# Linear attention feeding an MLP on one core: 128-token chunks cut into 64-token halves with a state between, all attention products on 64x64 tiles

## The chip, the cores and the metric

One core of a Trainium2 chip. TensorE (PE, with PEld for the load of its stationary operand), VectorE (DVE), ScalarE (ACT), GpSimd (POOL) and the DMA queue of SyncE (SP) run side by side and wait for each other by semaphores. The metric is the device time of one execution in microseconds (us), lower is better; the value is the median of the runs.

## The reference

```python
# B, H, S, D = 4, 8, 768, 48; d_model = H*D = 384, d_ff = 2048
for t in range(S):
    cur = einsum('bhd,bhe->bhde', u * k[t], v[t])
    y[t] = einsum('bhd,bhde->bhe', r[t], state + cur)
    state = w[..., None] * state + einsum('bhd,bhe->bhde', k[t], v[t])
x = y as (B*S, H*D)
h = x @ w_in
out = (max(h, 0) + alpha * min(h, 0)) @ w_out
```

## The kernel before

**Attention.** The 768 tokens are cut into C = 6 chunks of L = 128, and the 8 heads into P = 4 pairs; one call of `attention(c, q, at)` treats pair q of chunk c for the four batches. Head g of a pair lies on partitions 64g to 64g+47. r and k (tile `raw`) are loaded transposed and scaled by powers of w (L310). `scores` (L350) makes 8 products of 48 x 128 by 48 x 128, which fill the two banks A0 and A1; ACT writes the diagonal into `base` (L357) and DVE copies the strict triangle of the scores over it under a mask (L361). `out` adds the old state's part (L397, L391 in chunk 1) and the scores' part (L402, L386) in the bank or banks of y, and `state_product` (L411) makes the k-by-v product of the chunk, with which DVE updates the state T (L479). k is scaled for it by `scale_k` (L420). ACT and DVE split y in a rounded part `xh` and the rest `xl` (L444, L445). The fp32 products stand in the trace as two matmul records each: 8 products are 16 records. From chunk 2 on, y lies in two banks, written from four quadrants of the array; in chunks 0 and 1 it is one bank. The last chunk makes no state product.

**MLP.** 96 steps (`STEPS`), each one block of 128 hidden rows (i) of one chunk (c): `m_in` makes 9 products of 128 x 128 by 128 x 512 into a bank `hp` (L492), ACT and DVE make the activation and its split (L498, L499, L502, L503), and `m_out` adds 9 products to the three banks acc0 to acc2 (L523), three steps later. `SEGMENTS` orders them: blocks 0 to 8 of chunk 0, then of chunk 1, then blocks 9 to 15 of both, then chunk after chunk. So steps 0 to 8 each need a new block of weights, step 9 is the first of chunk 1, and step 18 is the next that needs new weights. `weights(i)` turns a block's bits into `wh` and `wl` with ACT (L253, L263) and DVE (L255, L257, L260, L264).

**Order.** Nothing is issued in program order: each piece of work is added to a `Plan` with its engine, an estimated time and a rank, and `in_order` lists the pieces as a list scheduler would start them (lowest rank of those that are ready). The engines then execute that list in order. The rank of attention is `at`, counted in MLP steps: `begins[c] - before + space * q`, with before and space of 9 and 1.4 for chunk 1, 11 and 2.4 for chunk 2, and 16 and 3.5 beyond. `scores` has rank at, `out` and `state_product` one PE piece of rank at + 1. In chunk 1 the masked copy, the splits and the state update have rank -60, that is, they go first. PSUM has 8 banks with fixed roles: two hp, A0, A1, y, and acc0 to acc2.

Of the kernel before, what the change touches and what calls it, by code (L numbers as in the profile page):

```python
# [18 lines left out]
L = 128  # L19
# [4 lines left out]
HI = 64  # L24
# [5 lines left out]
SPACE = {1: (1.4, 9.0), 2: (2.4, 11.0)}  # L30
# [16 lines left out]

class Piece:
    def __init__(self, eng, us, fn, reads, writes, rank, kb):
        self.eng, self.us, self.fn, self.rank, self.kb = eng, us, fn, rank, kb  # L50
        self.uses = [(r, 0) for r in reads] + [(x, 1) for x in writes]
        self.after, self.behind = set(), set()
        self.start = self.end = None


class Plan:
# [3 lines left out]
    def __init__(self):  # L60
        self.pieces, self.groups, self.log = [], {}, {}
# [19 lines left out]
    def in_order(self):  # L81
# [20 lines left out]

        def ready(p):
            t = 0.0
            for q in p.after:
                t = max(t, q.end + (0.0 if q.eng == p.eng else 0.2 if q.eng == "PE" else 0.1))
            for q in p.behind:
                t = max(t, q.start + 0.001)
            return t
# [5 lines left out]
        while any(waiting.values()):  # L115
            t, e = min((max(free[e], min(x[0] for x in ps)), e) for e, ps in waiting.items() if ps)
            at, p = min((x for x in waiting[e] if x[0] <= t + 0.02), key=lambda x: (x[1].rank, number[x[1]]))
            waiting[e].remove((at, p))
# [16 lines left out]
def rwkv_prelu_kernel(ctx: ExitStack, tc, rk, vkr, wP, uP, u, wall, alpha, w, r_all, k_all, v_all, oT):  # L135
# [25 lines left out]
    one, ones, ident = fixed([128, 2], "one"), fixed([128, 128], "ones"), fixed([128, 128], "ident")  # L161
    strict = fixed([128, 128], "strict", U8)
    utab, alph = fixed([128, H, D], "utab"), fixed([128, NF], "alph")
# [3 lines left out]
    wtok, w128, unit = fixed([128, H, D], "wtok"), fixed([112, P], "w128"), fixed([112, 65], "unit")  # L167

    T = [fixed([112, B, D], f"T{m}") for m in range(P)]
# [5 lines left out]
    bank = pb([128, NT], "acc2")  # L175

# [22 lines left out]
    add("POOL", 0.3, lambda: nc.gpsimd.tensor_copy(strict(), ones()), r=[ones], w=[strict], rank=-99)  # L199
    add("DVE", 0.1, lambda: nc.vector.memset(unit(), 0.0), w=[unit], rank=-100)  # L200
# [16 lines left out]
    def token_table():  # L217
        rows, pt = sb([112, P, L], "g", 3), pb([128, P, 2, HI], "A1")
# [4 lines left out]
        for m in range(P):  # L223
            add("PE", 0.15, lambda m=m: nc.tensor.transpose(
                pt()[:, m].rearrange("p g e -> p (g e)")[:, 0:112], rows()[:, m], ident()[0:112, 0:112]),
                r=[(rows, m), ident], w=[(pt, m)], rank=-30)
        add("DVE", 0.4, lambda: nc.vector.tensor_copy(
            wtok().rearrange("p (m g) e -> p m g e", g=2), pt()[:, :, :, 0:D]), r=[pt], w=[wtok], rank=-30)
# [52 lines left out]
    def attention(c, q, at):  # L281
        first, last = c == 0, c == C - 1

        r, k0 = (sb([112, B, L], *(("o", 2) if first and q == P - 1 else ("raw", 6)))
                 for _ in range(2))
        v, k = sb([128, 2 * B, D], "v", 4), sb([128, 2 * B, D], "kk", 3)
        n = 2 * B * D
        early = -99 + 0.1 * q if first else at - 7
        for j, t in enumerate((r, k0)):
# [3 lines left out]
             -98 + 0.2 * q if first else early + 0.1 * q + 0.15)  # L293

        def k_load():
            load(k, lambda: nc.sync.dma_start(k().rearrange("p x e -> p (x e)"), vkr[c, q, :, n:2 * n]), 192,
                 -20 + q if first else early + 0.1 * q + 0.2, [first_v[P - 1]] if first else [])

        if first:
            first_k.append(k0)  # L300
            first_v.append(v)
            if q == P - 1:
                raw_weights(0, -97, [k0])
                raw_weights(1, -95, [v])
        else:
            k_load()


        for j, (t, tab) in enumerate(((r, lambda: W[q]()[:, None, 0:L]), (k0, lambda: W[q]()[:, None, L - 1::-1]))):
            add("DVE", 0.72, lambda t=t, tab=tab: nc.vector.tensor_tensor(  # L310
                out=t(), in0=t(), in1=tab().broadcast_to([112, B, L]), op=ALU.mult),
                r=[W[q]], w=[t], rank=10 * q + j - 90 if first else at - 2)


        cu = sb([128, 2, B], "cu", 2)
        if c < 2:
            prod = sb([112, B, L], "g", 3)
            add("DVE", 0.7, lambda: nc.vector.tensor_tensor(out=prod(), in0=r(), in1=k0(), op=ALU.mult),
                r=[r, k0], w=[prod], rank=10 * q - 88 if first else at - 3)
            sums, cols = (pb([128, 2 * B], "y"), slice(0, 8)) if c else (bank, slice(8 * q, 8 * q + 8))  # L320
            mine = sums if c else (sums, q)

            def c_sum():
                for b in range(B):
                    nc.tensor.matmul(sums()[:, cols][:, 2 * b:2 * b + 2], prod()[:, b], uw()[:, q], start=True,  # L325
                                     stop=True, skip_group_check=True)

            add("PE", 1.0, c_sum, r=[prod, uw], w=[mine], rank=at - 0.2 - 40 * first - 20 * (c == 1))
            add("ACT", 0.2, lambda: nc.scalar.activation(cu(), sums()[:, cols].rearrange("p (b g) -> p g b", g=2), AF.Copy), r=[mine],
                w=[cu], rank=at - 1)  # L330
        else:
            rt = sb([128, 2 * B, D], "rr", 2)
            load(rt, lambda: nc.sync.dma_start(rt().rearrange("p x e -> p (x e)"), vkr[c, q, :, 2 * n:]), 192,
                 early + 0.1 * q + 0.2, [wh[0]])
            add("POOL", 1.2, lambda: nc.gpsimd.tensor_tensor(out=rt(), in0=rt(), in1=k(), op=ALU.mult), r=[k] + ([wh[12]] if c == 2 else []), w=[rt],  # L335
                rank=at - 2)
# [6 lines left out]


        A = [pb([128, B, L], f"A{g}" if not first or q % 2 == 0 else f"acc{g}") for g in range(2)]

        def scores():
            for b in range(B):
                for g in range(2):
                    nc.tensor.matmul(A[g]()[:, b], k0()[half(g), b], r()[half(g), b], start=(b == 0),  # L350
                                     stop=(b == B - 1), skip_group_check=True)

        add("PE", 1.1, scores, r=[r, k0], w=A, rank=10 * q - 90 if first else at)
        base = [sb([128, B, L], "base", 4) for _ in range(2)]
        for g in range(2):
            for b in range(B):
                add("ACT", 0.39, lambda g=g, b=b: nc.scalar.activation(  # L357
                    base[g]()[:, b], ident(), AF.Copy, scale=cu()[:, g, b:b + 1]), r=[cu, ident], w=[(base[g], b)],
                    rank=at - 0.9 if c != 1 else -50)
        for g in range(2):  # L360
            add("DVE", 0.75, lambda g=g: nc.vector.copy_predicated(  # L361
                base[g](), strict()[:, None, :].broadcast_to([128, B, L]), A[g]()), r=[strict, A[g]], w=[base[g]],
                rank=10 * q - 76 + g if first else at - 1.5 if c != 1 else -60)

        U, plain = None, c < 2
        if plain:
            y = pb([112, B, L], "y" if not first or q % 2 == 0 else "hp", 1 if not first or q % 2 == 0 else 2)
            if not first:  # L370
                U = mine = pb([112, B * D], "A0")
        else:
            y = [pb([112, 2 * 2 * L], "y"), pb([112, 2 * L], "A1")]
            U, mine = y[0], (y[0], "U")
            y_of = [(y[0], "y"), y[1]]

        def u_rows(rows):
            return U()[rows].rearrange("p (b e) -> p b e", b=B) if plain else \
                U()[rows, 2 * L:2 * L + B * D].rearrange("p (b e) -> p b e", b=B)

        def out():
            if plain:
                for b in range(B):
                    for g in range(2):
                        rows, x = (slice(0, HI) if g == 0 else half(g)), g * B + b
                        nc.tensor.matmul(y()[rows, b], v().rearrange("p x e -> p (x e)")[  # L386
                            :, x * D:x * D + rows.stop - rows.start], base[g]()[:, b], start=b == 0,
                            stop=first and b == B - 1, skip_group_check=True)
                for b in () if first else range(B):
                    for g in range(2):  # L390
                        nc.tensor.matmul(y()[half(g), b], T[q]()[half(g), b], r()[half(g), b], start=False,  # L391
                                         stop=(b == B - 1), skip_group_check=True)
                return
            for j in range(2):
                for g, o in ((0, 0), (1, 1), (0, 1), (1, 0)):
                    b = j + 2 * (g ^ o)
                    nc.tensor.matmul(y[g]()[half(o), j * L:(j + 1) * L], T[q]()[half(g), b], r()[half(g), b],  # L397
                                     start=(j == 0), stop=False, skip_group_check=True)
            for j in range(2):
                for g, o in ((0, 0), (1, 1), (1, 0), (0, 1)):  # L400
                    b = j + 2 * (g ^ o)
# [355 lines left out]
```

## Time and profile before

| | |
|---|---|
| median of 3 runs | 526.18 us (524.97 to 528.55) |
| profiled execution, span from first to last instruction | 523.0 us |
| the profiled execution's own time | not listed apart; the median lies 3.2 us above its span |
| PE busy | 509.0 us, 97% of the span |
| DVE busy | 321.0 us, 61% |
| ACT busy | 241.8 us, 46% |
| granted TensorE clock, mean | 0.991 |
| chain that ended last | 93% PE; lines L523 and L492 (the MLP) 38% each |

A high share of an engine is an average over stages; which engine sets the end of a stage is read from the stretches of the span and from the chain of work that ended last.

### The profile page before, as it was taken

What the parts mean: (1) busy time and instruction counts of PE and PEld (TensorE: products, weight loads), DVE (VectorE), ACT (ScalarE), POOL (GpSimd) and SP (SyncE); (2) the same over time, 40 slices, a digit from 0 to 9 for tenths busy, and PEclk for the clock granted to TensorE, in tenths of its full rate; (3) what the DMA queues carried; (4) which work ended last, traced back from release to release, by engine and by line L of the source; (5) the groups of instructions that cost most, each with busy time, mean ns of one, the idle gap of its engine ahead of it and who ended that gap; (6) DMA issues with size and microseconds to landing.
All of it is one profiled execution on the core that took longest, in us unless ns stands there. A gap on an engine that the chain in (4) does not pass through costs nothing.

```text
span 523.0 us, 8426 instructions
## 1 busy us (share of the span) xinstructions
PE 509.0 (97%) x3280; PEld 404.2 (77%) x3280; DVE 321.0 (61%) x513; ACT 241.8 (46%) x525; POOL 38.3 (7%) x45
## 2 busy tenths in 40 slices
PE   7989899999999999999999999999999999999995
PEld 6867677888878777877777777877777778888884
DVE  7799899999455866846764655564544443333331
ACT  3756556677455353543452643543534332432222
POOL 1000011001010112110110101120000000000000
PEclk9799999999999999999999999999999999999998
DMA  7964756552131551431211341220020000100001
GB/s 239 265 216 134 227 178 206 190 172 91 65 102 44 173 180 33 150 92 54 60 49 28 114 107 39 63 82 1 35 92 1 1 2 0 61 0 1 0 1 65
DMA packets 24877, 47.22 MB, mean 90 GB/s; under 512 B 4096, under 2 KB 12416, under 8 KB 24832
## 3 DMA queue, kind: packets, MB, share of 16 engines
q1 hardware_dynamic: 24832, 46.62, 28.3%
q8 instruction: 28, 0.46, 0.4%
q14 instruction: 17, 0.14, 0.1%
HBM read 37.96 MB, written 6.29 MB: 85 GB/s over the span
## 4 chain that ended last, share of the span: by engine, by line
PE 93%; DVE 3%; ACT 1%; DMA 1%; issue 1%; SPq 0%; DVEq 0%; ACTq 0%
PE acc L523 38%; PE hp L492 38%; PE A L350 5%; PE y L402 2%; PE y L397 2%; PE y L386 1%; PE A L402 1%; PE y L411 1%; PE acc L583 1%; PE acc L325 1%; DVE raw L310 1%; PE y L391 1%; DMA raw<-rk 1%; PE acc L350 1%; DVE base L361 1%
## 5 line engine op out<-in xcount | busy, mean ns | idle before, releaser
L499 DVE SCALAR_TENSOR_TENSOR g<-hp,alph,g 128x512 f32<-128x512 f32 x96 | 71.9, 749 | 126.8 <-ACT g L498 126.4
L498 ACT ACTIVATE g<-hp 128x512 f32<-128x512 f32 x96 | 57.3, 597 | 160.1 <-PE hp L492 159.7
L492 PE MATMUL hp<-xh,wh 128*128 128x512 f32 x288 | 116.6, 405 | 1.7 <-DMA xh<-xh 1.7
L492 PE MATMUL hp<-xl,wh 128*128 128x512 f32 x288 | 113.9, 396 | 0.0
L492 PE MATMUL hp<-xh,wl 128*128 128x512 f32 x288 | 113.9, 395 | 0.0
L503 DVE TENSOR_TENSOR gl<-g,gh 128x512 fp32r<-128x512 f32 x96 | 67.4, 702 | 39.4 <-ACT gh L502 39.0
L502 ACT ACTIVATE gh<-g 128x512 fp32r<-128x512 f32 x96 | 60.4, 630 | 61.3 <-DVE g L499 61.0
L523 PE MATMUL acc<-gh,wh 128*128 128x512 f32 x288 | 85.1, 402 | 0.1
L523 PE MATMUL acc<-gh,wl 128*128 128x512 f32 x288 | 83.3, 396 | 0.0
L523 PE MATMUL acc<-gl,wh 128*128 128x512 f32 x288 | 83.2, 396 | 0.0
L492 PEld LDWEIGHTS hp<-xh,wh 128*128 128x128 f32 x288 | 54.1, 188 | 16.2 <-issue 2.5
L492 PEld LDWEIGHTS hp<-xl,wh 128*128 128x128 f32 x288 | 54.1, 188 | 13.0
L523 PEld LDWEIGHTS acc<-gl,wh 128*128 128x128 f32 x288 | 54.0, 188 | 13.1
L523 PEld LDWEIGHTS acc<-gh,wl 128*128 128x128 f32 x288 | 54.0, 188 | 13.0
L492 PEld LDWEIGHTS hp<-xh,wl 128*128 128x128 f32 x288 | 54.1, 188 | 11.9
L523 PEld LDWEIGHTS acc<-gh,wh 128*128 128x128 f32 x288 | 52.6, 188 | 13.7 <-ACT gh L502 0.7
L357 ACT ACTIVATE base<-ident,cu 128x128 f32<-128x128 f32 x192 | 60.2, 390 | 1.0 <-DVE cu L341 0.7
L335 POOL TENSOR_TENSOR rr<-rr,kk 128x384 f32<-128x384 f32 x16 | 17.8, 1114 | 312.5 <-DMA kk<-vkr 207.2
L310 DVE TENSOR_TENSOR raw<-raw,W 112x512 f32<-112x512 f32 x46 | 35.3, 786 | 1.7 <-DMA raw<-rk 1.7
L361 DVE COPY_PREDICATED base<-strict,A 128x512 f32<-128x512 uint8 x44 | 30.5, 731 | 4.6 <-ACT base L357 2.5
L350 PEld LDWEIGHTS A<-raw 48*128 48x128 f32 x352 | 22.0, 192 | 7.5 <-issue 6.2
L350 PE MATMUL A<-raw 48*128 48x128 f32 x352 | 26.2, 290 | 0.0
(90 smaller groups left out, 416.5 us busy)
## 6 DMA issues: line engine op xcount, KB each, us to landing
wraw<-wall SPq DMA_DIRECT2D x16, 768.0 KB, 4.5
raw<-rk SPq DMA_DIRECT2D x46, 224.0 KB, 3.6
v<-vkr SPq DMA_DIRECT2D x24, 192.0 KB, 3.7
kk<-vkr SPq DMA_DIRECT2D x24, 192.0 KB, 3.5
rr<-vkr SPq DMA_DIRECT2D x16, 192.0 KB, 2.4
oT<-o SPq DMA_DIRECT2D x12, 256.0 KB, 2.0
oT<-g SPq DMA_DIRECT2D x6, 256.0 KB, 2.5
xh<-xh SPq DMA_DIRECT2D x36, 32.0 KB, 2.0
```

The source lines that it names most:

```text
L310: add("DVE", 0.72, lambda t=t, tab=tab: nc.vector.tensor_tensor(out=t(), in0=t(), in1=tab().broadcast_to([112, B, L]), op=ALU.mult), r=[W[ ...
L335: add("POOL", 1.2, lambda: nc.gpsimd.tensor_tensor(out=rt(), in0=rt(), in1=k(), op=ALU.mult), r=[k] + ([wh[12]] if c == 2 else []), w=[rt] ...
L350: nc.tensor.matmul(A[g]()[:, b], k0()[half(g), b], r()[half(g), b], start=(b == 0), stop=(b == B - 1), skip_group_check=True)
L357: add("ACT", 0.39, lambda g=g, b=b: nc.scalar.activation(base[g]()[:, b], ident(), AF.Copy, scale=cu()[:, g, b:b + 1]), r=[cu, ident], w=[ ...
L361: add("DVE", 0.75, lambda g=g: nc.vector.copy_predicated(base[g](), strict()[:, None, :].broadcast_to([128, B, L]), A[g]()), r=[strict, A[ ...
L402: nc.tensor.matmul(y[g]()[half(o), j * L:(j + 1) * L], v()[:, g * B + b], base[g]()[:, b], start=False, stop=(j == 1), skip_group_check=True)
L492: nc.tensor.matmul(hp(), a[i]()[:, k], x[c]()[:, k], start=(k == 0 and j == 0), stop=(k == NK - 1 and j == 2))
L498: add("ACT", 0.6, lambda: nc.scalar.activation(g(), hp(), AF.Copy), r=[hp], w=[g], rank=n - 100)
L499: add("DVE", 0.75, lambda: nc.vector.scalar_tensor_tensor(out=g(), in0=hp(), scalar=alph()[:, i:i + 1], in1=g(), op0=ALU.mult, op1=ALU.max ...
L502: add("ACT", 0.64, lambda: nc.scalar.activation(gh(), g(), AF.Copy), r=[g], w=[gh], rank=n - 100)
L503: add("DVE", 0.73, lambda: nc.vector.tensor_tensor(out=gl(), in0=g(), in1=gh(), op=ALU.subtract), r=[g, gh], w=[gl], rank=n - 99)
L523: nc.tensor.matmul(banks[k](), a[i]()[:, NK + k], x(), start=(begin and j == 0), stop=(end and j == 2))
```

## The change

Chunk 0 stays as it is. From chunk 1 on, r and k are scaled over 64 tokens, and a chunk is treated as two halves with a state between: the state T0 before the chunk gives the first half's output, T1 = T0 * w^64 + (first half's k-by-v product) the second half's, and only 64 x 64 blocks of scores are made. For a pair and four batches that is 16 products of scores (into A0 and A1, columns 0 to 255), 16 of k by v (into the same banks from column 256; 8 in the last chunk, which needs T1 alone), 16 through the states and 16 through the scores, each on one of four 64 x 64 tiles of the array.

A PE piece `burst(i, was, at)` makes, for the pair ahead (`was`), the products through the states and the half of those through the scores whose row half j equals the head g, and then, for pair i, the k-by-v products and the scores. The other half of the products through the scores ("crossed") writes the same two y banks from the other row half of the array. It is a PE piece of its own, which waits for an ACT instruction that reads two elements of y (`seen`). So a pair's output is made in the next pair's burst. Chunk 1's bursts are 1.5 steps apart from 0.5 on, chunk 2's 3.2 from 17 on, later ones 4 from begins - 18.5 on; the ones of chunks 1 and 2 begin with a burst of products alone, and the last of chunk 1 and of chunk 5 end with one of outputs alone.

The two hp banks, A0, A1 and y become five banks that the scheduler hands out (`Bank`): a burst takes four at once. A second table `whalf` of powers of w over 64 tokens is made at the start (8 ACT copies, 4 transposes on PE, one DVE copy). The masked copies are 128 x 256 in place of 128 x 512, a pair has two state updates (one in the last chunk, which had none), and chunk 1's y is split in four parts of 48 x 256 as in the later chunks, with ranks near at in place of -60. `scale_k` is now done in the last chunk too. `rr` has one buffer in place of two. A first product of a chunk's MLP step waits for all of xh and xl only in chunks 1 to 5.

```diff
+class Bank:
+    def __init__(self, plan, group, bufs):
+        self.plan, self.slot, self.group, self.bufs = plan, None, group, bufs
...
+    plan.banks += [ps.tile([128, NT], F32, name=f"bank{i}") for i in range(5)]
...
+        def soonest(p):
+            if not p.takes:
+                return []
+            return sorted((x, i) for i in range(len(held)) if (x := open_from(i)) is not None)[:len(p.takes)]
...
+    def half_table():
+        rows, pt = sb([112, P, L], "g", 3), psum()
+        for m in range(P):
+            for j in range(2):
+                add("ACT", 0.3, lambda m=m, j=j: nc.scalar.activation(
+                    rows()[:, m, HI * j:HI * (j + 1)], W[m]()[:, L - 1:HI - 1:-1], AF.Copy, scale=W[m]()[:, L:L + 1]), r=[W[m]],
+                    w=[(rows, (m, j))], rank=-21)
...
+            A = [psum() for _ in range(2)]
...
+            def products():
+                kt = k().rearrange("p x e -> p (x e)")
+                for b in range(B):
+                    for j in range(halves):
+                        for g in range(2):
+                            x, s = g * B + b, slice(HI * j, HI * (j + 1))
+                            rows = slice(HI * g, HI * g + (D if g and b else HI))
+                            nc.tensor.matmul(A[j]()[rows, 256 + b * D:256 + (b + 1) * D],
+                                                 kt[s, x * D:x * D + rows.stop - rows.start], v()[s, x],
+                                                 start=(b == 0), stop=False, skip_group_check=True)
...
+                        for j in range(2):
+                            s = slice(HI * j, HI * (j + 1))
+                            nc.tensor.matmul(A[g]()[s, b * HI:(b + 1) * HI], k0()[half(g), b, s], r()[half(g), b, s],
+                                             start=(g >= halves and b == 0), stop=(b == B - 1),
+                                             skip_group_check=True)
+        if before:
+            (c0, q0), r0, v0, base0, *states0 = before
+            y = [psum() for _ in range(2)]
...
+            def through_state():
+                for j, t in enumerate(states0):
+                    for e in range(2):
+                        for g in range(2):
+                            for b in (e, e + 2):
+                                nc.tensor.matmul(where(g, b, j), t()[half(g), b],
+                                                 r0()[half(g), b, HI * j:HI * (j + 1)], start=(j == 0 and e == 0),
+                                                 stop=False, skip_group_check=True)
+
+            def through_scores(crossed):
+                for e in (1, 0) if crossed else (0, 1):
+                    for g in (1, 0) if crossed else (0, 1):
+                        j = g ^ crossed
+                        s = slice(HI * j, HI * (j + 1))
+                        for b in (e + 2, e):
+                            nc.tensor.matmul(where(g, b, j), v0()[s, g * B + b], base0()[s, g, b], start=False,
+                                             stop=(crossed == 1 and e == 0), skip_group_check=True)
...
+        first = add("PE", (0.7 if before else 0.1) + (0.8 if now else 0.1), run, r=uses, w=writes, rank=at)
+        if before:
+
+            seen = add("ACT", 0.2, lambda: nc.scalar.activation(seen_y(), y[1]()[0:1, L + HI - 1:L + HI + 1], AF.Copy),
+                       r=[y[1]], rank=at - 200)
+            seen.soon[first] = 0.75
+            add("PE", 0.3, lambda: through_scores(1), r=[v0, base0], w=y, rank=at - 200)
+        if now:
+            for g in range(2):
+                add("DVE", 0.42, lambda g=g: nc.vector.copy_predicated(
+                    base()[:, g], strict2()[:, None, :].broadcast_to([128, B, HI]),
+                    A[g]()[:, 0:256].rearrange("p (b t) -> p b t", b=B)), r=[strict2, A[g]],
+                    w=[(base, (g, b)) for b in range(B)], rank=at - 0.5)
...
+            for j in range(halves):
+                t = sb([112, B, D], "T", 9)
+                add("DVE", 0.42, lambda t=t, j=j, of=T[q]: nc.vector.scalar_tensor_tensor(
+                    out=t(), in0=of(), scalar=W[q]()[:, L:L + 1], in1=u_rows(A[j], 256), op0=ALU.mult,
+                    op1=ALU.add), r=[A[j], T[q], W[q]], w=[t], rank=at - 0.4)
...
-    for c in range(1, C):
-        space, before = SPACE.get(c, (3.5, 16.0))
-        for q in range(P):
-            at = begins[c] - before + space * q
-            jobs.append((at, 3, lambda c=c, q=q, at=at: attention(c, q, at)))
+    bursts = []
+    for i, (c, q) in enumerate(pairs):
+        at = {1: 0.5 + 1.5 * q, 2: 17.0 + 3.2 * q}.get(c, begins[c] - 18.5 + 4 * q)
+        bursts.append((i, None if c < 3 and q == 0 else i - 1, at))
+        if c == 1 and q == P - 1:
+            bursts.append((None, i, at + 1.5))
+    bursts.append((None, len(pairs) - 1, at + 4))
```

## Rows read from the trace of the kernel before

**Rows 1.** The page: span, busy time of the engines, one transfer (us to landing last).
```profile
span 523.0 us, 8426 instructions
...
PE 509.0 (97%) x3280; PEld 404.2 (77%) x3280; DVE 321.0 (61%) x513; ACT 241.8 (46%) x525; POOL 38.3 (7%) x45
...
xh<-xh SPq DMA_DIRECT2D x36, 32.0 KB, 2.0
```
**Rows 2.** Stretches: length, then busy us (instructions) of PE, PEld, DVE, ACT, POOL.
```profile
28.00:93.00 65.00, 60.44 (x531) 46.73 (x529) 62.26 (x93) 37.46 (x79) 4.66 (x4) 1.00 0.62 200
93.00:131.00 38.00, 38.00 (x165) 30.59 (x164) 37.31 (x54) 27.51 (x51) 2.21 (x2) 1.00 0.43 142
131.00:511.00 380.00, 380.00 (x2347) 301.39 (x2346) 198.69 (x320) 157.59 (x344) 29.64 (x26) 1.00 0.18 56
```
**Rows 3.** DVE in order of time: start us, us, instruction.
```profile
57.87 0.74 DVE L361 COPY_PREDICATED base<-strict,A 128x512 f32<-128x512 uint8 x1 [1.67 <-ACT base L357]
...
89.02 0.55 DVE L255 TENSOR_SCALAR wx<-wx 128x768 uint32<-128x768 uint32 x1
...
90.15 0.94 DVE L264 TENSOR_TENSOR wl<-wx,wh 128x768 fp32r<-128x768 f32 x1
```
**Rows 4.** The chain that ended last, to 95 us: start us, us, what.
```profile
72.60 1.02 PE y L386 x15
...
74.62 0.59 PE A L411 x14
...
90.35 1.09 PE A L350 x16
91.44 3.69 PE hp L492 x15
```
**Rows 5.** The chain, 156 to 165 us, a pair of chunk 2.
```profile
156.86 1.09 PE A L350 x16
157.96 2.29 PE acc L523 x9
...
162.35 0.24 PE y L397
...
163.95 0.45 PE y L411 x14
164.39 0.66 PE acc L523 x2
```
**Rows 6.** The whole chain's longest pieces, on both sides of an output of chunk 5.
```profile
387.19 2.10 PE hp L492 x9
390.88 2.30 PE acc L523 x9
```
**Rows 7.** PE in order of time, the state's part of one pair's output.
```profile
162.43 0.27 PE L397 MATMUL y<-raw,T 48*48 48x128 f32 x1
...
162.45 0.27 PE L397 MATMUL A<-raw,T 48*48 48x128 f32 x1
162.54 0.27 PE L397 MATMUL y<-raw,T 48*48 48x128 f32 x1
```
**Rows 8.** Groups of instructions by line and form: busy us, mean ns of one.
```profile
L361 DVE COPY_PREDICATED base<-strict,A 128x512 f32<-128x512 uint8 x44 | 30.5, 731 | 4.6 <-ACT base L357 2.5 <-PE A L350 2.1
L445 DVE TENSOR_TENSOR xl<-y,xh 48x256 fp32r<-48x256 f32 x32 | 13.5, 421 | 0.5
L445 DVE TENSOR_TENSOR xl<-y,xh 112x512 fp32r<-112x512 f32 x6 | 4.1, 682 | 2.3 <-ACT xh L444 2.3
L479 DVE SCALAR_TENSOR_TENSOR T<-T,w,A 112x192 f32<-112x192 f32 x4 | 1.6, 409 | 0.0
L498 ACT ACTIVATE g<-hp 128x512 f32<-128x512 f32 x96 | 57.3, 597 | 160.1 <-PE hp L492 159.7
L499 DVE SCALAR_TENSOR_TENSOR g<-hp,alph,g 128x512 f32<-128x512 f32 x96 | 71.9, 749 | 126.8 <-ACT g L498 126.4
L329 ACT ACTIVATE cu<-y 128x8 f32<-128x8 f32 x4 | 0.7, 175 | 7.8 <-PE y L325 7.8
```

More of the change, by code (lines that the diff above doesn't have):

```diff
@@ L279, in lower, with splits, refs, to @@
                 add("SP", 0.45, dma, r=[top[name]], w=[(t, (k, g))], rank=-40 if c == 0 else -8, kb=32)
[L281 to L286, printed above, removed]
+    def splits(k, h, l, src, view, out_rows, cols, parts, us, rank):
+        def refs(t):
+            return [(t, (k, p)) for p in parts]
+        def to(t):
+            return t()[out_rows, cols] if k is None else t()[out_rows, k, cols]
+        add("ACT", us, lambda: nc.scalar.activation(to(h), view(), AF.Copy), r=[src], w=refs(h), rank=rank)
+        add("DVE", us + 0.1, lambda: nc.vector.tensor_tensor(out=to(l), in0=view(), in1=to(h), op=ALU.subtract),
+            r=[src] + refs(h), w=refs(l), rank=rank)
+    def x_tiles(c, q):
+        if q == 0:
+            for t, name in ((xh, "xh"), (xl, "xl")):
+                t[c] = sb([128, NK, NT], name, 2, F32R)
+                top[name] = sb([112, NT], name + "0", 1, F32R)
+        return (top["xh"], top["xl"], None) if q == 0 else (xh[c], xl[c], q - 1)
+    def inputs(c, q, r, k0, v, k, early):
         n = 2 * B * D
-        early = -99 + 0.1 * q if first else at - 7
         for j, t in enumerate((r, k0)):
@@ L311, in attention @@
                 out=t(), in0=t(), in1=tab().broadcast_to([112, B, L]), op=ALU.mult),
-                r=[W[q]], w=[t], rank=10 * q + j - 90 if first else at - 2)
+                r=[W[q]], w=[t], rank=10 * q + j - 90)
         cu = sb([128, 2, B], "cu", 2)
[L316 to L323, printed above, removed]
-                for b in range(B):
[L325 to L330, printed above, removed]
+        diagonal(q, r, k0, cu, bank, slice(8 * q, 8 * q + 8), (bank, q), 10 * q - 88, -90.2 + q, -51 + q)
@@ new lines, in first_chunk, with scores @@
+        A = [psum() if q % 2 == 0 else pb([128, NT], f"acc{g}") for g in range(2)]
+        def scores():
+            for b in range(B):
+                for g in range(2):
+                    nc.tensor.matmul(A[g]()[:, b * L:(b + 1) * L], k0()[half(g), b], r()[half(g), b], start=(b == 0),
+                                     stop=(b == B - 1), skip_group_check=True)
+        add("PE", 1.1, scores, r=[r, k0], w=A, rank=10 * q - 90)
+        base = [sb([128, B, L], "gl" if q % 2 else "base", 3) for _ in range(2)]
@@ new lines, in first_chunk, with out @@
+        y = psum()
+        def out():
+            for b in range(B):
+                for g in range(2):
+                    rows, x = (slice(0, HI) if g == 0 else half(g)), g * B + b
+                    nc.tensor.matmul(y()[rows, b * L:(b + 1) * L], v().rearrange("p x e -> p (x e)")[
+                        :, x * D:x * D + rows.stop - rows.start], base[g]()[:, b], start=b == 0,
+                        stop=b == B - 1, skip_group_check=True)
+        add("PE", 1.0, out, r=[v] + base, w=[y], rank=10 * q - 90)
@@ L354, in attention @@
-        base = [sb([128, B, L], "base", 4) for _ in range(2)]
+        base = sb([128, 2, B, HI], "base", 3)
         for g in range(2):
             for b in range(B):
[L357 to L363, printed above, removed]
@@ L367, in attention @@
[L367 to L379, printed above, removed]
@@ L381, in out, with burst @@
-        def out():
-            if plain:
+                add("ACT", 0.32, lambda g=g, b=b: nc.scalar.activation(
+                    base()[:, g, b], ident2(), AF.Copy, scale=cu()[:, g, b:b + 1]), r=[cu, ident2],
+                    w=[(base, (g, b))], rank=at - 0.9)
+        add("DVE", 0.56, lambda: scale_k(k, whalf, q), r=[whalf], w=[k], rank=at - 1.6)
+        return r, k0, v, k, base
+    def burst(i, was, at):
+        now = None if i is None else pairs[i]
+        before = None if was is None else made.pop(was)
+        uses, writes = [], []
+        if now:
+            c, q = now
+            r, k0, v, k, base = prepare(c, q, at)
+            halves = 2 if c < C - 1 else 1
+            A = [psum() for _ in range(2)]
+            uses += [r, k0, v, k]
+            writes += A
+            def products():
+                kt = k().rearrange("p x e -> p (x e)")
+                for b in range(B):
+                    for j in range(halves):
+                        for g in range(2):
+                            x, s = g * B + b, slice(HI * j, HI * (j + 1))
[3 more added lines that the diff above has]
+                                                 start=(b == 0), stop=False, skip_group_check=True)
@@ L383, in out @@
                 for b in range(B):
                     for g in range(2):
[L385 to L401, printed above, removed]
-                    nc.tensor.matmul(y[g]()[half(o), j * L:(j + 1) * L], v()[:, g * B + b], base[g]()[:, b],
-                                     start=False, stop=(j == 1), skip_group_check=True)
@@ L405, in state_product @@
-        def state_product():
-            kt, vt = k().rearrange("p x e -> p (x e)"), v()
-            for b in range(B):
-                for g in range(2):
-                    rows, x = slice(HI * g, HI if g == 0 else HI + D), g * B + b
-                    nc.tensor.matmul(u_rows(rows)[:, b], kt[:, x * D:x * D + rows.stop - rows.start], vt[:, x],
-                                     start=(b == 0), stop=(b == B - 1), skip_group_check=True)
-        def both():
-            out()
-            state_product()
@@ L607, in rwkv_prelu_kernel @@
         table(m)
-    states = [attention(0, q, -50 + q) for q in range(P)]
+    states = [first_chunk(q) for q in range(P)]
     token_table()
```

271 lines of the change are left out of this document (176 added, 95 removed).

## The prediction

> **What bounds the kernel now.** I read the shares first: PE is busy 97% of the span, DVE 61% [rows 1]. An average over stages says little, so the stretches come next [rows 2]. From 131 to 511 us PE is busy 380.00 of 380 us and DVE 198.69: there every TensorE microsecond taken out shortens the kernel. From 93 to 131 PE is full as well, and DVE nearly so (37.31 of 38). From 28 to 93 us both are nearly full, DVE 62.26 and PE 60.44 of 65, and the question is who sets the pace. The weights answer it: DVE ends block 8's conversion at 90.15 + 0.94 = 91.09 [rows 3], and the product of step 8 that needs it starts at 91.44 [rows 4]. So up to step 9 DVE delivers just in time and PE fills the gaps; from there on PE alone sets the end. I treat the two parts apart, with the border at 93 us.
>
> **The part from 93 us on: what a pair costs PE now.** A piece of 9 MLP products takes 2.10 us, and 2.29 or 2.30 when it follows attention [rows 5, 6], so leaving attention costs 0.19. Scores: 1.09 + 0.19 = 1.28. Outputs and state product: from 162.35 to 164.39, 2.04, + 0.19 = 2.23 [rows 5]. That is 3.51 for each of the 12 pairs of chunks 2 to 4. In chunk 5 there is no state product: from 387.19 + 2.10 = 389.29 to 390.88, 1.59, + 0.19 + 1.28 = 3.06 for 4 pairs [rows 6]. Sum 12 x 3.51 + 4 x 3.06 = 54.4; one scores piece stands ahead of 93 us (at 90.35) [rows 4], so 53.1 lie in this part.
>
> **What a pair will cost.** The four-quadrant products show the pattern: three of a round's four records start at 162.43 to 162.45, the next round at 162.54 [rows 7]. Four tiles work at once and a round of 128 columns lasts 0.11. The k-by-v products, with 48 columns on two tiles, end 14 records in 0.45 [rows 5], 0.064 a round; their weights are up to 64 columns wide. A new round (64 columns of each) is not in this trace: half of 0.11 is 0.055, the k-by-v round 0.064; I take 0.06, between them, since the new products share something with each. What comes on top of the rounds now: scores, 8 rounds of two = 0.88, of 1.28, leaves 0.40; outputs and state, 4 x 0.11 + 8 x 0.11 + 8 x 0.06 = 1.80 of 2.23, leaves 0.43. I take 0.40 for each entry and exit. The new pair makes 64 products, 128 records, on four tiles: 8 rounds through the states, 4 + 4 through the scores, 8 for k by v (still 8 in chunk 5, where the half left uses two tiles), 8 for the scores: 32 x 0.06 + 0.40 = 2.32. Sixteen of them and one more entry for the last output alone: 37.5. **Gain 53.1 - 37.5 = 15.6**; with 0.055 it is 18.1, with 0.064 13.5.
>
> **The wait that is added.** The crossed products wait for the ACT read of y, and behind them on PE stand all MLP products. The read may start when 12 rounds are done and have arrived: some 0.2 + 0.72 + 0.27 (the duration of a small product [rows 7]) = 1.2 after the burst's start; such a read takes 0.18 [rows 8], 1.4. The rounds queued ahead of the crossed ones (28) last until 0.2 + 1.68 = 1.9. So 0.5 us of products cover the wait, and an MLP copy of 0.60 that ACT has in hand [rows 8] would overrun it by a tenth only. I take nothing; if the cover fails, or MLP work is listed between the two parts, one more entry of 0.40 is due, at 17 outputs 6.8 us. Behind the read on ACT stand the MLP's copies of hp, at most the same half microsecond.
>
> **Banks.** A burst takes four of the five, so m_in has one hp until y and A are free. A lone hp is free after ACT's and DVE's reads, 0.60 + 0.75 = 1.35 [rows 8], while m_out's 2.10 pass on PE; nothing is lost unless DVE lags by over 0.75. A burst's own DVE reads of PSUM are two masked copies of 128 x 256 (from the slope between 421 and 682 ns over 256 elements, 0.73 - 0.26 = 0.47 each), two state updates of 0.41 and four splits of 0.42, together 3.4 us [rows 8], within a step of 4.2. DVE has 181 us idle from 131 on [rows 2], which also takes the last chunk's extra scaling and updates. The single `rr` buffer is filled, used and freed within one burst's distance; nothing.
>
> **The part up to 93 us.** PE loses work: a pair of chunk 1 now costs 1.28 + (74.62 + 0.59 - 72.60 + 0.19 = 2.80) = 4.08 [rows 4, 5] against 2.32; 4 x 1.76 - 0.40 = 6.6. But DVE sets the pace, and it gets more: per pair the masked copies -0.52, a second state update +0.41, four splits of 0.42 in place of one of 0.68, +1.00 [rows 8]; 0.89 x 4, and the copy of the second table, at most 0.68: +4.2. Against it: 0.55 of block 9's conversion runs here though nobody needs it before step 18, and 1.67 of DVE's idle time hung on a late PE product [rows 3]; PE, now ahead, can make a further m_out (2.10) while it waits. On the other side chunk 1's last splits (4 x 0.42) and the transfer behind them (2.0 [rows 1]) now stand directly before step 9. 4.2 - 0.6 - 1.7 - 2.1 = -0.2, + up to 3.7 less the 2.1 of step 8's own products: +1.4 at the worst of these. I take 0. The ends are -6.6 (DVE does not set the pace after all) and +6 (none of the reliefs comes). The second table's 8 ACT copies find ACT idle 27 of 65 us [rows 2]; the finer wait of step 0 moves nothing that DVE doesn't hold.
>
> **Sum.** 523.0 - 15.6 + 0 = 507.4 us of span. The median of the runs lies 526.18 - 523.0 = 3.2 above this span, so **510.6 us**.
>
> **A rule against it.** Rows 7 show starts on different tiles 0.01 apart. The Trainium skill ("TensorE: Matmul & The Clock Gate", section "Wait — 56ns, not 53.3ns?") says that matmuls never start closer than about 25 ns, however small. By it 128 records would last 3.2 + 0.40 = 3.6 us, and nothing would be won. The starts on different tiles contradict it over three records; over a long row of records no run here shows it.
>
> **The rivals.** (1) *Slower: PE can't feed four small tiles.* In rows 5 and 7 the mean is never below 27 ns a record (four in 0.11), even where starts cluster. If that is a limit of issue and not of the tiles, the pair costs 128 x 0.027 + 0.40 = 3.9 (112 records, 3.4, in chunk 5): 60.9 against 53.1, +8, the early part +1, so 523 + 9 + 3.2 = 535. It decides from (3.51 - 0.40) / 128 = 24 ns a record. For it: no row is below. Against it: in rows 7 a gap of 0.09 follows each cluster, as when tiles are still busy. Chance 0.12. The page's rule above is this rival. (2) *The wait or the banks take part of it back*: the order is written from estimates, and a burst that needs four free banks and an ACT read may leave PE idle or split the burst, 0.4 to 0.8 per output: +7 to +13, 517 to 523. For it: ACT and DVE run MLP work first. Against: half a microsecond of cover. Chance 0.18. (3) *The early part grows* by 6, since DVE is full there: 516.6. Chance 0.12. (4) *The early part shrinks with PE's work*, -6.6: 504. For it: PE is on the chain for most of it. Against: the weights that come 0.35 us ahead of use. Chance 0.13.
>
> **How the numbers follow.** The forecast, 506 to 515, has 0.45. A change of 1%, 5.3 us, is about what a measurement can tell from none. Faster by over 1% (under 520.9): the forecast, (4), (3) less a little and two thirds of (2): 0.45 + 0.13 + 0.11 + 0.12 = 0.81. Within 1%: 0.01 + 0.06 + 0.03 = 0.10. Slower: 0.09, all of (1). The range goes from 500 (rounds of 0.055 with the shorter early part, 510.6 - 2.5 - 6.6 = 501.5) to 524, the upper end of (2); it leaves out (1) and little else.
>
> **What would show it.** After the change, the 32 score records of a pair should take about 0.5 us (four a round) and a whole burst about 2 us, with MLP pieces back to back around it and PE still full from 100 us on; step 9 should begin near 93 us. Records 27 ns apart through the whole burst mean rival 1. PE idle before the crossed products, ended by ACT, or MLP products between a burst and its crossed part, mean rival 2. A first product of steps 8 or 9 that waits for DVE or for the transfer, past 96 us, means rival 3. The prediction would be wrong above all if four tiles share more than the trace's wide rounds let see.

## Result and the profile after

The changed kernel takes **498.68 us** (median of 4 runs, 498.5 to 501.65) against 526.23 (524.97 to 528.55): ratio 0.9486, 95% interval 0.9452 to 0.952. I had forecast 510.6 with 500 to 524: the sign is right, the gain is 27.5 us where I had 15.6 (measured from the median shown before the prediction), and the time lies just below the range. The profiled execution took 498.5 us, 1.8 above its span of 496.7, at a mean granted clock of 0.987 (before 0.991).

The page of the changed kernel, beside [rows 1]:
```profile
span 496.7 us, 11103 instructions
...
PE 477.7 (96%) x4563; PEld 390.2 (79%) x4563; DVE 322.1 (65%) x550; ACT 242.5 (49%) x565; POOL 45.1 (9%) x49
...
PE acc L661 38%; PE bank L628 36%; PE bank L569 2%; PE bank L579 2%; PE bank L550 2%; PE bank L543 2%; DMA wraw<-wall 1%; DVE wx L333 1%; DVE xl L362 1%; DMA raw<-rk 1%; DVE wl L337 1%; DVE wx L330 1%; DVE g L637 1%; PE acc L473 1%; DVE raw L496 1%
```
The lines are new: L628 is `m_in`, L661 `m_out`; a burst is L569 (through the states), L579 (through the scores, the crossed half too), L543 (k by v) and L550 (scores); L592 reads `seen_y`; L598, L605 and L362 are the masked copy, the state update and the split. Over the span PE has 31.3 us less to do, DVE 1.1 more.

The stretches, with the columns of [rows 2] and its first two borders:
```profile
28.00:93.00 65.00, 55.72 (x780) 43.29 (x781) 63.53 (x107) 41.88 (x99) 2.92 (x2) 0.97 0.64 199
93.00:131.00 38.00, 38.00 (x227) 31.09 (x226) 37.38 (x58) 25.36 (x50) 5.08 (x4) 1.00 0.44 141
131.00:485.00 354.00, 354.00 (x3321) 290.89 (x3320) 198.84 (x341) 155.72 (x361) 34.35 (x26) 1.00 0.20 61
```
From 93 us on PE is still busy without a gap, so what TensorE saves there is saved in the end. Up to 93 us PE fell from 60.44 to 55.72, but DVE went from 62.26 to 63.53 and the end of this part hardly moved.

PE in order of time: a wait for a bank, the lone output that ends chunk 1, the first product of step 9 (92.41), a burst of chunk 3, a `m_in`:
```profile
68.84 0.47 PE L628 MATMUL bank<-xh,wh 128*128 128x512 f32 x1 [3.42 <-DVE T L605]
...
83.06 0.66 PE L569 MATMUL bank<-raw,T 48*48 48x64 f32 x32
83.54 0.41 PE L579 MATMUL bank<-base,v 64*48 64x64 f32 x16
84.59 0.44 PE L579 MATMUL bank<-base,v 64*48 64x64 f32 x16 [0.64 <-ACT seen_y L592]
...
92.41 0.40 PE L628 MATMUL bank<-xh,wh 128*128 128x512 f32 x1
...
222.03 0.66 PE L569 MATMUL bank<-raw,T 48*48 48x64 f32 x32
222.52 0.41 PE L579 MATMUL bank<-base,v 64*48 64x64 f32 x16
222.74 0.57 PE L543 MATMUL bank<-v,kk 64*64 64x48 f32 x30
...
223.19 0.60 PE L550 MATMUL bank<-raw 48*64 48x64 f32 x28
...
223.67 0.41 PE L579 MATMUL bank<-base,v 64*48 64x64 f32 x14
224.01 0.97 PE L661 MATMUL acc<-gh,wh 128*128 128x512 f32 x3
224.82 0.85 PE L661 MATMUL acc<-gh,wl 128*128 128x512 f32 x3
225.51 0.86 PE L661 MATMUL acc<-gl,wh 128*128 128x512 f32 x3
226.21 0.40 PE L628 MATMUL bank<-xh,wh 128*128 128x512 f32 x1
226.44 0.39 PE L628 MATMUL bank<-xh,wl 128*128 128x512 f32 x1
226.67 0.39 PE L628 MATMUL bank<-xl,wh 128*128 128x512 f32 x1
```
The burst is 128 records from 222.03 to 224.01 (eight of them in the lines left out), with the crossed part directly behind the scores and no idle time. Only the lone output at 83.06 shows the wait for `seen_y`. The MLP products at 226.21 to 226.67 start 0.23 us apart.

The chain, with pieces that answer to [rows 6]:
```profile
49.54 6.64 DMA wraw<-wall
...
64.26 0.83 DVE wl L337
65.10 0.87 DVE wx L333
66.32 1.18 DVE raw L496 x2
67.50 0.87 DVE wl L337
...
389.72 0.59 PE bank L569 x32
...
391.68 2.29 PE acc L661 x9
393.96 2.04 PE bank L628 x9
396.01 2.06 PE acc L661 x9
```
Up to 90 us mostly DVE and a transfer of weights stand on it. Behind a burst an `m_out` takes 2.29, then 2.04 and 2.06 alternate where all pieces took 2.10 before. **That is the part of the gain that I had not priced.**

### The profile page after: what moved, and what is told of

It reads as the page before. It is cut to its first block, busy times and chain, and to the rows that moved or that the text cites. A ratio compares the mean times of both kernels' runs of the same rounds, so it can differ in the third digit from the quotient of the medians.

```text
span 496.7 us, 11103 instructions
## 1 busy us (share of the span) xinstructions
PE 477.7 (96%) x4563; PEld 390.2 (79%) x4563; DVE 322.1 (65%) x550; ACT 242.5 (49%) x565; POOL 45.1 (9%) x49
## 4 chain that ended last, share of the span: by engine, by line
PE 84%; DVE 8%; ACT 3%; DMA 2%; issue 1%; SPq 0%; DVEq 0%; ACTq 0%
PE acc L661 38%; PE bank L628 36%; PE bank L569 2%; PE bank L579 2%; PE bank L550 2%; PE bank L543 2%; DMA wraw<-wall 1%; DVE wx L333 1%; DVE xl L362 1%; DMA raw<-rk 1%; DVE wl L337 1%; DVE wx L330 1%; DVE g L637 1%; PE acc L473 1%; DVE raw L496 1%
## 5 line engine op out<-in xcount | busy, mean ns | idle before, releaser
L637 DVE SCALAR_TENSOR_TENSOR g<-bank,alph,g 128x512 f32<-128x512 f32 x96 | 72.0, 750 | 110.0 <-ACT g L636 108.5
L636 ACT ACTIVATE g<-bank 128x512 f32<-128x512 f32 x96 | 57.3, 597 | 141.0 <-PE bank L628 139.1
L628 PE MATMUL bank<-xh,wh 128*128 128x512 f32 x288 | 113.6, 395 | 3.4 <-DVE T L605 3.4
L628 PE MATMUL bank<-xh,wl 128*128 128x512 f32 x288 | 112.3, 390 | 0.4 <-DVE wl L337 0.3
L628 PE MATMUL bank<-xl,wh 128*128 128x512 f32 x288 | 112.1, 389 | 0.0
L661 PE MATMUL acc<-gh,wh 128*128 128x512 f32 x288 | 83.6, 397 | 1.6 <-ACT gh L640 1.6
L661 PE MATMUL acc<-gl,wh 128*128 128x512 f32 x288 | 83.2, 396 | 0.0
L661 PE MATMUL acc<-gh,wl 128*128 128x512 f32 x288 | 81.7, 391 | 0.0
L628 PEld LDWEIGHTS bank<-xh,wh 128*128 128x128 f32 x288 | 54.1, 188 | 15.8 <-ACT wx L326 3.8
L628 PEld LDWEIGHTS bank<-xh,wl 128*128 128x128 f32 x288 | 54.1, 188 | 12.6 <-DVE wl L337 1.3
L661 PEld LDWEIGHTS acc<-gl,wh 128*128 128x128 f32 x288 | 54.1, 188 | 12.1
L628 PEld LDWEIGHTS bank<-xl,wh 128*128 128x128 f32 x288 | 54.0, 188 | 11.7
L661 PEld LDWEIGHTS acc<-gh,wl 128*128 128x128 f32 x288 | 53.9, 188 | 11.6
L661 PEld LDWEIGHTS acc<-gh,wh 128*128 128x128 f32 x288 | 52.6, 188 | 13.2 <-ACT gh L640 1.9
L518 ACT ACTIVATE base<-ident,cu 128x64 f32<-128x64 f32 x160 | 41.4, 337 | 1.1 <-DVE cu L513 1.0
L362 DVE TENSOR_TENSOR xl<-bank,xh 48x256 fp32r<-48x256 f32 (+2 forms) x85 | 37.2, 438 | 3.5 <-ACT xh L361 1.7
```

The lines of the kernel that those rows point to most:

```text
L362: add("DVE", us + 0.1, lambda: nc.vector.tensor_tensor(out=to(l), in0=view(), in1=to(h), op=ALU.subtract), r=[src] + refs(h), w=refs(l), r ...
L518: add("ACT", 0.32, lambda g=g, b=b: nc.scalar.activation(base()[:, g, b], ident2(), AF.Copy, scale=cu()[:, g, b:b + 1]), r=[cu, ident2], w ...
L628: nc.tensor.matmul(hp()[:, :], a[i]()[:, k], x[c]()[:, k], start=(k == 0 and j == 0), stop=(k == NK - 1 and j == 2))
L636: add("ACT", 0.6, lambda: nc.scalar.activation(g(), hp()[:, :], AF.Copy), r=[hp], w=[g], rank=n - 100)
L637: add("DVE", 0.75, lambda: nc.vector.scalar_tensor_tensor(out=g(), in0=hp()[:, :], scalar=alph()[:, i:i + 1], in1=g(), op0=ALU.mult, op1=A ...
L661: nc.tensor.matmul(banks[k](), a[i]()[:, NK + k], x(), start=(begin and j == 0), stop=(end and j == 2))
```

## The experiments

The first product of step 9 starts at 93.6 us before and at 92.4 after. From it to the end of the span is 523.0 - 93.6 = 429.4 us before and 496.7 - 92.4 = 404.3 after: 25.1, where I had 15.6. I split each run there: "step 9 at" and "from step 9" below are of its profiled execution.

**Does the address of a tile set the pace of the MLP?** In the program built from the kernel before, the tiles that the MLP products read as moving operand (xh, xl, gh, gl) lie 32 bytes short of a multiple of 256 from the weights, per partition. In the changed one the small tile `seen_y` (32 bytes) lies ahead of them, and xh, xl and gh are at a multiple of 256, gl 32 short of one. A pad alone moves addresses and leaves every engine's instructions and their order as they are:

```diff
     flag = fixed([1, 1], "flag", I32)
+    fixed([1, 8], "pad")      # before_pad32, after_pad32
+    fixed([1, 16], "pad")     # after_pad64
```


> The kernel before with one unused 32-byte tile more, which moves the MLP's moving tiles (xh, xl, gh, gl) from an address that is 32 modulo 64 bytes to one that is 0. Theory A (the address sets the pace of the MLP products): nine products in a row take 2.04 to 2.05 us in place of 2.10, about 1480 to 1728 products gain 6.6 ns each, 514.8 to 516.4 us. Theory B (the pace comes from the new order and the new banks): 526 us, 2.10 us.

> The changed kernel with the same 32 bytes more: xh, xl and gh now lie at 32 modulo 64, gl alone at 0. Theory A: the mean distance of MLP products rises from 228.4 to some 232.3 ns, +6.5 to +7.6 us, 505 to 506.5; the products with gl become the fast ones. Theory B: 498.7, gl stays the slow one.

> A control: the changed kernel with 64 bytes more, so that every tile is moved but no address changes modulo 64. Theory A: 498.7, unchanged. If any shift of the tiles matters: another time.

The chain of the kernel before with the pad:
```profile
151.41 2.28 PE hp L493 x9
153.69 2.04 PE acc L524 x9
```
Of the changed kernel with a pad of 32 bytes:
```profile
311.01 2.09 PE acc L662 x9
313.11 2.09 PE bank L629 x9
```
An unused 32-byte tile makes the kernel before 516.78 us (515.44 to 518.66), ratio 0.9809 (0.9763 to 0.9855), and takes most of that from the changed one: 507.98 (504.59 to 509.71), 0.9625 (0.9577 to 0.9673). From step 9 they take 420.1 and 410.6. The pad of 64 bytes was meant as a control that changes nothing; it gave 501.98 (500.83 to 503.01), 0.9539 (0.9498 to 0.958), an interval that overlaps the changed kernel's, and from step 9 406.3, 2.0 more. A burst lasts 1.98 us in all three changed kernels. So the addresses do it, in the MLP products, but the rule with which I began, a period of 64 bytes, falls.

**Which distance?** Two small tiles were made wider (the program uses the same slices of them; `ok` lies ahead of all moving tiles, `w2` behind gl and ahead of the others), or the weights were moved along with the moving tiles:
```diff
+        ok = plan.buf(lambda: wk.tile([128, 32], F32, name="ok", bufs=1)[:, 0:NF + P], "ok", 1)
+        w2 = plan.buf(lambda: wk.tile([112, 16], F32, name="w2", bufs=1)[:, 0:P], "w2", 1)
```
This is after_all64; after_all128 has 32 in place of the 16, after_all256 has 64. after_wpad64 has a `fixed([1, 16], "pad")` behind `uw`, ahead of the weights.

> The changed kernel with two small tiles widened (ok to 128 bytes, w2 to 64), so that gl too lies at 0 modulo 64. Theory A: the 288 products with gl gain 6.6 ns each, -1.9 us, 496.8. Theory B: 498.7.

> The changed kernel with the small tiles ok and w2 widened to 128 bytes each, so that xh, xl, gh and gl all lie at the same place modulo 128 bytes as the weights (64). If the distance of moving tile and weights modulo 128 sets the pace (zero in the kernel before with 32 bytes more, whose products are all 227 ns apart): 226.7 to 227.2 ns throughout, some 2 us less than the changed kernel, 496.5. If what was seen is only a matter of 64 bytes: as in the run with 64-byte alignment, 231.7 ns, 504 to 505.

> The changed kernel with 64 bytes more ahead of the weights, so that weights, xh, xl and gh all move from 64 to 0 modulo 128. If only their distance counts: 228.4 ns and 498.7 us as in the changed kernel. If the moving tiles' own address counts: as with 64 bytes between weights and moving tiles, 230.0 ns and 501 to 502 us.

> The changed kernel with ok and w2 widened (to 128 and 256 bytes), so that gl too lies at a distance of 0 modulo 256 from the weights, as xh, xl and gh do already. In all kernels so far products were 227 ns apart where every moving tile had that distance, 233 where all were 32 off, and 229 to 235 where distances of 64 or 128 took part. If that is the rule: 226.7 to 227.2 throughout, 2 to 2.5 us less than the changed kernel. If more address bits decide: 229 or more for products with gl, and no gain.

The second column is how many bytes the moving tiles lie past (+) or short of (-) a multiple of 256 from the weights. The last one is the mean distance of starts of MLP products that follow each other directly, over all of them from step 9 on.

| kernel | xh, xl, gh; gl | us (range) | from step 9 | ns |
|---|---|---|---|---|
| before | -32; -32 | 526.23 | 429.4 | 233.3 |
| before_pad32 | 0; 0 | 516.78 | 420.1 | 227.2 |
| after | 0; -32 | 498.68 | 404.3 | 228.5 |
| after_pad32 | +32; 0 | 507.98 | 410.6 | 232.6 |
| after_pad64 | +64; +32 | 501.98 | 406.3 | 230.1 |
| after_all64 | +64; 0 | 504.98 (503.92 to 507.13) | 409.1 | 231.7 |
| after_all128 | +128; 0 | 507.62 (504.95 to 507.97) | 409.4 | 232.1 |
| after_wpad64 | 0; -32, weights and tiles moved by 64 | 500.84 (499.11 to 503.54) | 404.3 | 228.5 |
| after_all256 | 0; 0 | 498.77 (496.34 to 502.27) | 402.3 | 227.0 |

The chain of after_all256, where `m_out` too takes 2.04:
```profile
305.74 2.04 PE bank L628 x9
307.78 2.04 PE acc L661 x9
309.82 2.04 PE bank L628 x9
```
64 and 128 bytes off are slow as well, which I had not expected of either; moving weights and tiles together by 64 bytes changes nothing from step 9 on, so it is the distance, not the place. all256 does what a period of 256 says in the products (2.0 us less from step 9), but its profiled execution came to step 9 only at 98.2, and in the time the 2 us can't be told: ratio 0.946 (0.9432 to 0.9488). Product by product, the distance of its own tile alone doesn't decide. In the changed kernel products with gl, 32 short, follow each other every 234.5 ns, most others every 227, and in after_all256 those with gl take 226.9. But gl lies at 0 in after_pad32, after_all64 and after_all128 too, and its products are 231.9, 232.9 and 233.3 ns apart there. What is shown is 227 throughout where all four tiles lie at 0; why the other layouts average 228 to 233 stays open.

**Do four tiles work at once?** The same products, listed so that neighbours take turns on two tiles in place of four, in the k-by-v products and in the scores (`products` in the diff):
```diff
-                for b in range(B):
-                    for j in range(halves):
+                for j in range(halves):
+                    for b in range(B):
                         for g in range(2):
...
-                for b in range(B):
-                    for g in range(2):
+                for g in range(2):
+                    for b in range(B):
                         for j in range(2):
```


> The changed kernel with the loops of its k-by-v products and scores turned, so that two 64x64 tiles alternate where four did; the same products, the same records. If four tiles work at once, as the forecast has it: 8 rounds more for the scores and, but for chunk 5, 8 more for k by v, at 0.057 us: +0.91 a burst for 12 bursts, +0.46 for four, 511 to 512 us, up to 515 with chunk 1's. If records are limited by their issue and not by the tiles (rival 1): 498.7, unchanged.

507.68 us (502.42 to 509.62), 0.9624 (0.9562 to 0.9686); step 9 at 96.6; from step 9 410.1, 5.8 more, where I expected 12.8. PE in order of time:
```profile
228.41 0.66 PE L569 MATMUL bank<-raw,T 48*48 48x64 f32 x32
228.89 0.41 PE L579 MATMUL bank<-base,v 64*48 64x64 f32 x16
229.12 0.72 PE L543 MATMUL bank<-v,kk 64*64 64x48 f32 x26
...
230.76 0.50 PE L661 MATMUL acc<-gh,wh 128*128 128x512 f32 x1
```
The burst now lasts 2.35 in place of 1.98, and 2.26 in place of 1.96 in chunk 5, where only the scores are turned: 12 x 0.37 + 4 x 0.30 = 5.6 of the 5.8. So a limit of issue, which would have left the time as it was, is refuted again. But two tiles cost less than half of what I thought, and by the difference of 0.37 and 0.30 nearly nothing in the k-by-v products: a round of two tiles is not as long as a round of four. The edit also makes neighbours write into one PSUM bank where two took turns; tile and bank are not told apart.

**What sets the part up to step 9?** One more DVE instruction in each of the 16 weight blocks (the shift by 3 as 1 and 2); chunk 1's scaling of k and its product of r and k on GpSimd, on top of after_all256; and chunk 1's masked copies and state updates ahead of the weights, as before the change:
```diff
-        add("DVE", 0.56, lambda: nc.vector.tensor_scalar(bits(), bits(), 3, None, op0=ALU.logical_shift_left), w=[t],
+        add("DVE", 0.56, lambda: nc.vector.tensor_scalar(bits(), bits(), 1, None, op0=ALU.logical_shift_left), w=[t],
+            rank=need - 2 - 60 * (i == 0))
+        add("DVE", 0.56, lambda: nc.vector.tensor_scalar(bits(), bits(), 2, None, op0=ALU.logical_shift_left), w=[t],
...
+        add("POOL" if pool else "DVE", 1.6 if pool else 0.7, lambda: (nc.gpsimd if pool else nc.vector).tensor_tensor(
+            out=prod(), in0=r(), in1=k0(), op=ALU.mult), r=[r, k0], w=[prod], rank=prod_rank)
...
+            add("POOL", 1.2, lambda: scale_k(k, whalf, q, nc.gpsimd), r=[whalf], w=[k], rank=at - 1.6)
...
-                    w=[(base, (g, b)) for b in range(B)], rank=at - 0.5)
+                    w=[(base, (g, b)) for b in range(B)], rank=at - 0.5 - 60 * (c == 1))
...
-                    op1=ALU.add), r=[A[j], T[q], W[q]], w=[t], rank=at - 0.4)
+                    op1=ALU.add), r=[A[j], T[q], W[q]], w=[t], rank=at - 0.4 - 60 * (c == 1))
```


> The changed kernel with the shift by 3 in the weights' conversion made as a shift by 1 and one by 2: one DVE instruction of 0.55 us more for each block. Blocks 1 to 8 fall in the part before step 9. If DVE sets the pace there: step 9 begins some 4.4 us later, 502 to 503.5 us. If PE sets it: 498.7, step 9 where it was.

> The changed kernel once more, beside the next two: 498.5 to 501.7 as before; the spread of its runs tells how far the part up to step 9 varies by itself (92 to 97 us in the profiles so far).

> As after_all256, and in chunk 1 the scaling of k (0.55 us each) and the product of r and k (0.68 each) go from DVE to GpSimd, which is idle there: 4.9 us less on DVE up to step 9. If DVE sets the pace there: step 9 begins some 3 to 5 us earlier, 492 to 494 us. If PE, or the transfer of the weights, sets it: no earlier than after_all256.

> In chunk 1 alone the masked copies and the state updates get the rank at - 60 again, which the kernel before had, so VectorE takes them ahead of the weights and the banks of a burst come free sooner. In the trace of the changed kernel TensorE stands idle once, for 3.42 us up to 68.84, until a state update gives a bank free, while VectorE works on weights. Theory P, this wait for a bank is what the early part pays: the wait falls under 1 us, step 9 begins near 89 to 91 us in place of 92.4, and the time falls by 1 to 3 us to 495.5 to 497.5. Theory Q, VectorE has the same work in any order and the weights are as late as before: the idle time appears at another place, for weights, step 9 begins at 91.5 to 93.5, and the time stays at 498.7 within 1.5 us. Theory R, the weights now come later by the four instructions that pass them, some 1.7 us a pair: step 9 at 94 to 96 and a time of 500 to 502. From step 9 on all expect 404.3 us.

after_again is the changed kernel once more, beside them. Stretches of after_two_shifts:
```profile
28.00:108.00 80.00, 64.98 (x793) 50.10 (x791) 75.25 (x126) 43.84 (x104) 2.75 (x2) 0.87 0.51 162
```
of after_pool:
```profile
28.00:93.00 65.00, 55.09 (x765) 43.05 (x762) 59.26 (x97) 39.17 (x94) 15.20 (x10) 0.92 0.62 197
```
and of after_free_first, PE in order of time:
```profile
68.51 0.50 PE L628 MATMUL bank<-xh,wl 128*128 128x512 f32 x1 [0.69 <-DVE wl L337]
...
84.96 1.65 PE L661 MATMUL acc<-gh,wh 128*128 128x512 f32 x3 [2.80 <-ACT gh L640]
86.41 0.63 PE L628 MATMUL bank<-xh,wh 128*128 128x512 f32 x1
...
90.25 1.24 PE L661 MATMUL acc<-gh,wl 128*128 128x512 f32 x3
```

| kernel | us (range) | ratio (95%) | step 9 at | from step 9 |
|---|---|---|---|---|
| after_two_shifts | 512.35 (510.8 to 514.96) | 0.9744 (0.9702 to 0.9787) | 108.0 | 402.8 |
| after_again | 499.4 (498.01 to 500.87) | 0.9486 (0.9462 to 0.9509) | 92.0 | 404.3 |
| after_pool | 497.79 (496.15 to 500.02) | 0.9456 (0.9427 to 0.9484) | 94.0 | 401.8 |
| after_free_first | 501.11 (498.08 to 501.58) | 0.9491 (0.9458 to 0.9523) | 95.4 | 404.1 |

More DVE work does hurt: step 9 comes 15.6 us later, where I had 4.4; but the order of the list changed with it (nine MLP products more lie ahead of step 9, some 2 us), and the granted clock of that stretch is 0.87, so the size isn't DVE's alone. Less DVE work does not bring step 9 ahead of 92: after_pool has 4.3 us less busy up to 93 than the changed kernel and 1.7 less than after_all256 (60.93), on which it builds. In after_free_first the 3.42 us for a bank at 68.84 are gone, and as much comes back: PE waits 2.80 for an activation at 84.96, some 0.7 of it because DVE had other pieces first, and behind this idle time the granted clock is 0.50 (1.2 GHz) from 84.5 to 90.5, so that the `m_in` at 86.41 takes 3.84 until 90.25 where 2.04 is usual. So that wait for a bank was not what step 9 pays (theory P falls; step 9 and the time lie where theory R had them, though this time can't be told from that of after_again, and the clock has a share that R did not name).

One profile's "step 9 at" must be read with care. In the eight profiles of the changed kernel in which only addresses differ, or nothing, it lies between 92.0 and 98.2, and most of that is there when step 0 begins, at 28.6 to 34.6. The stretch up to 28 us of the changed kernel, then of after_all256:
```profile
0.00:28.00 28.00, 24.89 (x218) 21.17 (x218) 21.30 (x46) 17.12 (x54) 2.71 (x17) 0.88 0.80 236
0.00:28.00 28.00, 25.19 (x189) 21.56 (x191) 18.35 (x42) 14.12 (x44) 2.72 (x17) 0.76 0.77 235
```
A granted clock of 0.76 there goes with step 9 at 97.4 to 98.2 (after_pad32, after_wpad64, after_all256), one of 0.88 or 0.94 with 92.0 to 93.8 (the other five). From step 0 to step 9 all eight take 61.2 to 63.7 us; after_pool takes 64.3, after_free_first 67.1 and after_two_shifts 76.7. So moving DVE work away gained nothing in this stretch, and with more of it the stretch is 13 to 15.5 us longer, some 2 of them for the nine products. What exactly bounds it stays open; after_pool's median is the lowest of all, but not by more than the runs spread.

## Why the prediction was off, step by step

**The step that failed: a piece of 9 MLP products, 2.10 us, taken over unchanged.** It is the largest part of PE's work, and I priced only what the diff touches in the order of products. `seen_y`, which I had looked at as an ACT read and a wait, also moved every tile behind it by 32 bytes; without it xh, xl and gh would lie 32 short, as before. The pads show that this is worth 9.3 us from step 9 in the kernel before (429.4 to 420.1) and 6.3 in the changed one (404.3 to 410.6). Two kernels at equal distances, before_pad32 and after_all256, differ by 17.8 from step 9: that is the attention. The remaining 7.3 of the 25.1 is the faster MLP product. That some tiles came to lie better was luck: neither the prediction nor the edit aimed at it.

**A pair's burst.** Forecast 2.32, measured 1.98, + 0.19 to 0.23 for the piece behind it (2.29 against 2.06) = 2.2. The rounds are shorter: in the states' part of the burst at 222.03 they start 0.149, 0.205 and 0.260 us after its first record, 0.056 apart, next to the lower bound of 0.055, and 2.2 - 32 x 0.056 leaves 0.41 for entry and exit. Sixteen times 0.12 is 2, and 15.6 + 2 = 17.6 agrees with the 17.8. This term was mis-sized within its bounds.

**The added wait.** "I take nothing" held: no PE time is lost to ACT where products cover it; among 16 outputs from 131 us on, the crossed part follows the scores directly in 15, and in the last, where no next pair covers it, three MLP products were listed between. The other uncovered case, chunk 1's last output, shows the price: 0.64 of idle time at 84.59.

**Banks.** Right from 93 us on, wrong before: one `m_in` waits 3.42 for a state update that DVE puts behind weights and scalings. The 3.4 us of DVE reads within a step had no such queue in my sum. It cost nothing that could be shown, for the reason above.

**The part up to 93 us.** Step 9 at 92.4 instead of 93.6: 1.2 gained, taken as 0, and less than profiles of one program differ. That PE's 6.6 us do not come through was right: PE is 4.7 us less busy there. That DVE is what holds them is argued, not shown: more DVE work delays step 9, less does not advance it. My list of reliefs is not borne out by any run.

**The sum.** 507.4 - 1.2 - 2 - 7.3 - 0.2 (rounding) = 496.7 of span. To the median it is 2.0, where I carried 3.2 over from before; other executions of the kernel before lie 1.7 to 1.8 above their spans (524.55 and 522.8), so the profiled one was faster than the median.

**The rivals.** (1), issue at 27 ns a record, is refuted: 128 records in 1.98 us are 15.5 ns each. So is, for products on different tiles, the rule of the Trainium skill ("TensorE: Matmul & The Clock Gate", section "Wait — 56ns, not 53.3ns?") that starts never come closer than about 25 ns. This row of 128 contradicts it with its mean of 15.5. (2), 0.4 to 0.8 an output, did not come. (3) and (4) did not come in their full size. The low end of the range, 500, was made from short rounds and (4); no case in it had a faster MLP.

## What to carry to other kernels

When a change adds or removes a small tile, look at the addresses of the large ones before the sum is made: here 32 bytes were worth 6 to 9 us of 500, up to half of what the edit's attention gained (17.8). Compare two kernels at equal distances before the difference is put down to the edit. And where four small tiles take turns, price a round from the nearest round with the same width, not from the records' mean.

## What the hardware showed that I had not expected

- Products of 128 x 128 by 128 x 512 follow each other every 227.0 to 227.2 ns where all moving tiles lie a multiple of 256 bytes from the weights (after_all256, before_pad32), and every 233.3 where all are 32 short (before); with xh, xl and gh 32, 64 or 128 past it is 230.1 to 232.6 on average. The granted clock is 1.00 from 131 to 480 us in all of them.
- Four 64 x 64 tiles take 128 records in 1.98 us, 15.5 ns each; with the same products listed over two tiles at a time in two of four parts it is 2.35.
- A low granted clock in the first 28 us (0.76 against 0.88 to 0.94) went with a step 9 that came some 4 to 6 us later in profiles of programs that differ by addresses alone.
